# Spacing the weight halves between the chunk loads of a retention, soft-MoE and MLP kernel

## The chip, the cores and the metric

The kernel runs on one core of one Trainium2 chip. The metric is the device time of one execution in microseconds (us), the median of three runs; smaller is better. MB are 10^6 bytes, MiB 2^20.

## What is computed

Three layers follow each other on 4 x 768 = 3072 tokens of 512 features, all in 32-bit floats. The first is a retention layer of 8 heads of 64, written in the reference as a recurrence over time:

```python
for t in range(S):
    state = gamma[None, :, None, None] * state + np.einsum('bhd,bhe->bhde', k[:, :, t], v[:, :, t])
    y[:, :, t] = scale * np.einsum('bhd,bhde->bhe', q[:, :, t], state)
```

The second is a soft mixture of 8 experts with 4 slots each. Its logits are softmaxed over the tokens to make the slots' inputs, and over the slots to mix the experts' outputs:

```python
logits = x @ phi
d = softmax(logits, over tokens); slot_input = (d.T @ x).reshape(E, S_per_e, D)
slot_out[e] = np.maximum(slot_input[e] @ w1[e], 0.0) @ w2[e]
c = softmax(logits, over slots); x = c @ slot_out
```

The third is a plain MLP, `h = x @ w_in; g = h * sigmoid(1.702 h); out = g @ w_out`, with an inner width of 2048. The experts' weights `w1` (8 x 512 x 1024) and `w2` (8 x 1024 x 512) are 32 MiB together, by far the largest input.

## The kernel before

**The chunk loop.** The tokens are worked through in NI = 24 chunks of 128 (NC = 6 in each of 4 sequences). Chunk i has three inputs in DRAM: `ktv[i]` (k transposed and v, 512 KiB), `qt[i]` (q transposed, 256 KiB) and, for 12 of the chunks, `kt[i]` (k not transposed, 256 KiB; for the chunks in KTP the tensor engine transposes k itself, L221, and the last chunk of a sequence needs none). `stage_a` multiplies k by q (L210, tile sc), `stage_v` scales v on GpSimd (POOL), `stage_b` makes the chunk's output y from the running state and the chunk (L255, L259) and updates the state (L267), `stage_c` transposes the result (L280). Every fourth chunk closes a group, with logits (L312) and the token softmax. Iteration i of the loop runs `stage_a(i)`, `stage_b(i - 1)` and `stage_c(i - 2)`.

**The loads.** Nearly all transfers are issued by SyncE (SP), one after the other in program order, and an issue that has to wait for a buffer holds up everything behind it. Three sorts stand in that order: the chunk loads (`load_a(i + 2)` for ktv and qt, L185 and L187; `load_b(i + 1)` for kt, L199), the expert weights, and, later, the MLP's weights. `ktv` and `qt` have three buffers each, so that `qt[i + 2]` waits until the tensor engine has read `qt[i - 1]` in L255.

The expert weights come as 32 pieces of 1 MiB, in the order in which the experts use them: four pieces each of w1 of expert pair 0, w1 of pair 1, w2 of 0, w1 of 2, w2 of 1, w1 of 3, w2 of 2 and w2 of 3. 17 of these pieces (NW + NQ buffers, 14 and 3) are loaded during the chunk loop in 34 halves of 512 KiB (`load_half`, L123 and L128). The other 15 follow behind the loop (`load_piece`, L136; the very last in two halves again). Their buffers come free as the loop's tiles are closed and as the experts consume earlier pieces. Between the last ones stand the first halves of the MLP's `w_in` (L149) and `w_out` (L143).

How many halves each iteration issues, ahead of its own chunk loads, is set by one expression: in iteration i > 0, until `2 + i * 34 // 23` of them have been issued. That is three halves in iteration 1, then one or two in each, with the last one behind the loads of chunk 23.

**Behind the loop.** The slots' inputs are made (L475), then the four expert pairs run: `exp_w1` (L488, tile hp) and `exp_w2` (L513, tile eo), each 32 matmuls over four pieces. The last is `exp_w2(3)`, whose fourth piece is the last of the 32 to be loaded. Its result is copied out of PSUM in two halves, by ScalarE (L520) and VectorE (L521, tile os), transposed (L530, tile tq) and turned into the slots' outputs. From there the MLP runs on the tensor engine to the end (L644, L667, L730).

Of the kernel before, what the change touches and what calls it, by code (L numbers as in the profile page):

```python
# [24 lines left out]
NI = B * NC  # L25
# [8 lines left out]
NW = 14  # L34
NQ = 3
# [3 lines left out]
FULL = (2, 6, 7)  # L39
Q = 256  # L40
NWU = 3
I0 = 1
KTP = (0, 1, 2, 3, 8, 13, 16, 20)
BUD = 2.3
C1, C2 = 0.34, 0.6
# [4 lines left out]
def retention_soft_moe_mlp(  # L50
# [69 lines left out]
    def load_half(pool):  # L120
        if half:
            t, src = half.pop()
            nc.sync.dma_start(out=t[:, 2:4], in_=src[:, 2:4])  # L123
            return
        kind, e, k = pieces.pop()
        t = pool.tile([P, 4, 512], F32, tag="w", name=f"{kind}_{e}_{k}")
        src = (w1 if kind == "w1" else w2)[e, k].rearrange("p (j f) -> p j f", j=4)
        nc.sync.dma_start(out=t[:, 0:2], in_=src[:, 0:2])  # L128
        W[kind, e, k] = t
        half.append((t, src))  # L130
# [43 lines left out]
    def load_a(i):  # L174
        if i < NI:
            src = ktv[i].rearrange("p (a t) -> p a t", a=2)
            if i == 2:
                early.append(wp.tile([P, 4, 512], F32, tag="w", name="early"))
                ktv_t[i] = early[0][:, 0:2]
            else:  # L180
                ktv_t[i] = wt(f"ktv{i % 3}", [P, 2, 512], f"ktv{i}")
            if i < 2:
                nc.sync.dma_start(out=ktv_t[i][:, 0], in_=src[:, 0])
            else:
                nc.sync.dma_start(out=ktv_t[i], in_=src)  # L185
            qt_t[i] = wt(f"qt{(i + 1) % 3}", [P, NP, P], f"qt{i}")
            nc.sync.dma_start(out=qt_t[i], in_=qt[i].rearrange("p (a t) -> p a t", a=NP))  # L187
# [4 lines left out]
    def load_b(i):  # L192
        if i < NI and i % NC < NC - 1:
            if i == 3:
                t = early[0][:, i].rearrange("p (h d) -> p h d", h=H)
            else:
                t = wt(f"kt{(i - i // NC) % 3}", [P, H, D], f"kt{i}")
            if i not in KTP:
                nc.sync.dma_start(out=t, in_=kt[i].rearrange("p (h d) -> p h d", h=H))  # L199
            kt_t[i] = t  # L200
# [3 lines left out]
    def stage_a(i):  # L204
        q_, kv = qt_t[i], ktv_t[i]
        kT = kv[:, 0].rearrange("p (a t) -> p a t", a=NP)
        sc = [ps.tile([P, NP, P], F32, tag=f"sc{hh}", name=f"sc{hh}_{i}") for hh in range(2)]
        for a in range(NP):
            for hh in range(2):
                mm(sc[hh][:, a, :], lhsT=kT[hh * D:(hh + 1) * D, a, :], rhs=q_[hh * D:(hh + 1) * D, a, :],  # L210
                   start=True, stop=True)
        pt = [wt(f"pt{hh}{i % 2}", [P, NP, P], f"pt{hh}_{i}") for hh in range(2)]
        for hh in range(2):
            nc.vector.tensor_tensor(  # L214
                out=pt[hh], in0=sc[hh], in1=mask[:, None, :].to_broadcast([P, NP, P]), op=ALU.mult
            )
        p_t[i] = pt
        if i in KTP and i % NC < NC - 1:
            kp = ps.tile([P, NP, P], F32, tag="m", name=f"kp{i}", bufs=3)
            for a in range(NP):  # L220
                nc.tensor.transpose(kp[:, a, :], kT[:, a, :], ident)  # L221
            nc.scalar.copy(out=kt_t[i].rearrange("p h d -> p (h d)"), in_=kp.rearrange("p a t -> p (a t)"))

    def stage_v(i):
        c = i % NC
        v_ = ktv_t.pop(i)[:, 1].rearrange("p (h d) -> p h d", h=H)
        vt = wt(f"vt{i % 2}", [P, H, D], f"vt{i}")
        nc.gpsimd.tensor_tensor(
            out=vt, in0=v_, in1=vs[:, c, :, None].to_broadcast([P, H, D]), op=ALU.mult
        )  # L230
        vt_t[i] = vt
        if c == 0:
            tb_t[i] = tab
        else:
            tb_t[i] = wt("tb", [P, NP, P], f"tb{i}")
            nc.gpsimd.tensor_tensor(
                out=tb_t[i], in0=tab, in1=gsc[:, :, c, None].to_broadcast([P, NP, P]), op=ALU.mult
            )
# [3 lines left out]
    def stage_b(i):  # L242
        c = i % NC
        q_, vt, pt = qt_t.pop(i), vt_t.pop(i), p_t.pop(i)
        y = ps.tile([P, 2, 512], F32, tag="y", name=f"y{i}")

        def out_(a, hh):
            o = hh ^ (a & 1)
            return y[o * D:(o + 1) * D, a % 2, P * (a // 2):P * (a // 2) + P]

        if c > 0:
            for a in range(NP):
                for hh in range(2):
                    r = slice(hh * D, (hh + 1) * D)
                    mm(out_(a, hh), lhsT=s_sb[r, a, :], rhs=q_[r, a, :], start=(a < 2), stop=False,  # L255
                       skip_group_check=True)
        for a in range(NP):
            for hh in range(2):
                mm(out_(a, hh ^ (a & 1)), lhsT=vt[:, 2 * a + (hh ^ (a & 1)), :], rhs=pt[hh ^ (a & 1)][:, a, :],  # L259
                   start=(c == 0 and a < 2), stop=True, skip_group_check=True)  # L260
        if c < NC - 1:
            if c == 0:
                st_p[0] = ps.tile([P, NP, D], F32, tag="st", name=f"st{i}")
            st, k_ = st_p[0], kt_t.pop(i)
            for a in range(NP):
                for hh in range(2):
                    mm(st[hh * D:(hh + 1) * D, a, :], lhsT=k_[:, 2 * a + hh, :], rhs=vt[:, 2 * a + hh, :],  # L267
                       start=(c == 0 and a == 0), stop=True, skip_group_check=True)
            nc.scalar.copy(out=s_sb, in_=st)
        xT = xx.tile([P, NP, P], F32, tag="xT", name=f"xT{i}")  # L270
        nc.vector.tensor_tensor(
            out=xT.rearrange("p (s k) t -> p k s t", k=2), in0=y[:, :, 0:2 * P].rearrange("p k (s t) -> p k s t", s=2),
            in1=tb_t.pop(i).rearrange("p (s k) t -> p k s t", k=2), op=ALU.mult,
        )
        xT_t[i] = xT
# [23 lines left out]
    def stage_g1(g, part=False):  # L299
        if part in (True, False):  # L300
            lp = logits(g)
            if part:
                return lp
        else:
            lp = part
        softmax_stats(g, lp)
# [77 lines left out]
    def row_softmax(g):  # L384
        lp = ps.tile([P, 4, NS], F32, tag="m", name=f"rl{g}", bufs=3)
        nc.tensor.transpose(lp.rearrange("p j s -> p (j s)"), lT_t.pop(g), ident)
        rx = sm.tile([P, 4], F32, tag="rx", name=f"rx{g}")
        nc.vector.reduce_max(out=rx, in_=lp, axis=AX.X)
        ce = sm.tile([P, 4, NS], F32, tag="eT", name=f"ce{g}")
        nc.vector.tensor_tensor(out=ce, in0=lp, in1=rx[:, :, None].to_broadcast([P, 4, NS]), op=ALU.subtract)  # L390
        ex = sm.tile([P, 4, NS], F32, tag="ex", name=f"ex{g}", bufs=1)
        nc.scalar.activation(out=ex, in_=ce, func=AF.Exp)
        return ex
# [460 lines left out]
    with tc.manual_schedule():  # L854
# [18 lines left out]
        loaded = 0  # L873
        ex_t = {}
        for i in range(NI + 2):
            if i == 2:
                stage_b(1)
            if i < NI:
                stage_a(i)
                stage_v(i)  # L880
                while i > 0 and loaded < min(2 * (NW + NQ), 2 + i * 2 * (NW + NQ) // (NI - I0)):
                    load_half(wp if loaded < 2 * NW else wq)
                    loaded += 1
                load_b(i + 1)
                load_a(i + 2)
            if i >= 8 and i % 4 == 0 and i < NI:
                ex_t[i // 4 - 2] = row_softmax(i // 4 - 2)
            if i >= 9 and i % 4 == 1 and i < NI:
                row_norm(i // 4 - 2, ex_t.pop(i // 4 - 2))
            if 1 <= i <= NI and i != 2:  # L890
                stage_b(i - 1)
            if i >= 2:
                n = i - 1
                g = n // 4 - 1
                if i < NI + 1:
                    stage_c(i - 2)
                else:
                    lp = stage_g1(g, True)
                    stage_c(i - 2, True)
                    softmax_stats(g, lp)  # L900
                    combine1()
                    last_z = stage_g2(g)
                    stage_c2(i - 2)
                if n % 4 == 0 and i <= NI:
                    stage_g1(g)
                if n % 4 == 1 and n > 4:
                    stage_g2(g)
                if n % 4 == 2 and 4 < n < 22:
                    stage_g3(g)
# [337 lines left out]
```

## Time and profile before

| | us |
|---|---|
| median of three runs | 449.44 (449.42 to 450.48) |
| profiled execution, its own time | 451.76 |
| profiled execution, span from first to last instruction | 450.0 |
| tensor engine (PE) busy | 433.1 (96%) |
| VectorE / ScalarE / GpSimd busy | 333.4 / 205.3 / 47.9 |
| chunk loop, in that span | to about 115 |
| experts, in that span | about 121 to 159 |

The page divides the span in 40 slices of 11.25 us and gives for each the busy tenths of every engine, the tensor engine's granted clock and the rate of the DMA engines. The chain of waits is followed back from the last instruction, each step to what released it. A DMA in the chain lasts from its issue to its landing. All times "at 109.06" are us from the start of the span.

### The profile page before, as it was taken

The numbers are of one execution on the slowest core, as the hardware profiler recorded it, in microseconds if no ns is written. First come the engines' busy times: TensorE is split into PE (matmuls) and PEld (weight loads), VectorE is DVE, ScalarE is ACT, GpSimd is POOL, SyncE is SP. The second block draws the span as 40 slices with busy tenths as digits, with TensorE's granted clock in tenths as the row PEclk, the third lists the DMA queues.
The fourth block names the chain that finished last, engine by engine and source line by source line (L and its number), as shares of the span: only waits on it lengthen the run. The fifth ranks groups of instructions, "written<-read, shape, count | busy, mean of one in ns | idle before, by whom it ended". The sixth has DMA issues, their size and how long they took to land.

```text
span 450.0 us, 9917 instructions
## 1 busy us (share of the span) xinstructions
PE 433.1 (96%) x4105; PEld 359.9 (80%) x4105; DVE 333.4 (74%) x600; ACT 205.3 (46%) x351; POOL 47.9 (11%) x53
## 2 busy tenths in 40 slices
PE   8799998999999989999999999999999999999996
PEld 5687876877533367788888889999999999999995
DVE  2345665756456587987979689897797797988984
ACT  2232232322220166474656655655555555565530
POOL 3353543343100000000000000000000000000000
PEclk9999999999999999999999999999999999999999
DMA  8999999999899968687555502001301401311012
GB/s 300 407 365 408 389 371 407 344 407 325 328 411 411 380 228 281 182 299 268 181 194 188 184 5 94 1 1 47 129 14 47 141 1 49 140 48 46 23 74 93
DMA packets 27661, 92.38 MB, mean 205 GB/s; under 512 B 2864, under 2 KB 4288, under 8 KB 23264
## 3 DMA queue, kind: packets, MB, share of 16 engines
q1 hardware_dynamic: 27248, 91.24, 55.1%
q8 instruction: 32, 0.52, 0.5%
q10 hardware_dynamic: 288, 0.36, 0.3%
q0 software_dynamic: 80, 0.15, 0.1%
q14 instruction: 13, 0.11, 0.1%
HBM read 79.16 MB, written 12.58 MB: 204 GB/s over the span
## 4 chain that ended last, share of the span: by engine, by line
PE 81%; DMA 12%; DVE 3%; ACT 1%; issue 1%; POOL 1%; SPq 0%; DVEq 0%; POOLq 0%; ACTq 0%
PE P L730 35%; PE acc L667 18%; DMA qt<-qt_dram 10%; PE sc L210 4%; PE hb L696 4%; PE hp L488 3%; PE y L259 3%; PE eo L513 3%; PE y L255 2%; PE P L840 2%; PE xp L280 1%; PE op L370 1%; PE h L644 1%; DMA ktv_first<-ktv_dram 1%; PE st L267 1%
## 5 line engine op out<-in xcount | busy, mean ns | idle before, releaser
L691 DVE TENSOR_TENSOR forms<-forms 128x256 f32<-128x256 f32 (+1 forms) x93 | 47.6, 512 | 22.3 <-ACT forms L698 21.0
L698 ACT ACTIVATE forms<-hb 128x512 f32<-128x512 f32 x62 | 37.2, 599 | 54.7 <-PE hb L696 34.9
L667 PE MATMUL acc<-wo_hl,gh 128*128 128x512 f32 x192 | 59.8, 394 | 0.4 <-ACT gh L646 0.4
L730 PE MATMUL P<-bh,la 128*128 128x256 f32 x208 | 59.0, 284 | 0.0
L730 PE MATMUL P<-bl,ha 128*128 128x256 f32 x208 | 58.8, 283 | 0.0
L730 PE MATMUL P<-bh,ha 128*128 128x256 f32 x208 | 58.7, 282 | 0.0
L214 DVE TENSOR_TENSOR pt<-sc,ca_t 128x512 f32<-128x512 f32 x44 | 28.3, 685 | 24.5 <-PE sc L210 24.5
L730 PE MATMUL P<-bh,hs 128*128 128x256 f32 x156 | 44.1, 283 | 0.0
L730 PE MATMUL P<-bh,ls 128*128 128x256 f32 x156 | 44.1, 282 | 0.0
L730 PE MATMUL P<-bl,hs 128*128 128x256 f32 x156 | 44.0, 282 | 0.0
L667 PEld LDWEIGHTS acc<-wo_hl,gh 128*128 128x128 f32 x192 | 35.4, 188 | 8.1 <-issue 0.6
L730 PEld LDWEIGHTS P<-bl,ha 128*128 128x128 f32 x208 | 39.4, 189 | 1.2
L730 PEld LDWEIGHTS P<-bh,ha 128*128 128x128 f32 x208 | 39.4, 190 | 0.0
L730 PEld LDWEIGHTS P<-bh,la 128*128 128x128 f32 x208 | 39.4, 189 | 0.1
L691 DVE TENSOR_TENSOR la<-forms,ha 128x1024 fp32r<-128x1024 f32 x31 | 37.9, 1223 | 0.0
L667 PE MATMUL acc<-wo_hl,gl 128*128 128x512 f32 x96 | 37.4, 394 | 0.3 <-DVE gl L654 0.3
L714 ACT CAST ha<-forms 128x1024 fp32r<-128x1024 f32 x31 | 32.6, 1053 | 6.5 <-DVE forms L691 5.6
L646 ACT ACTIVATE gh<-h 128x512 fp32r<-128x512 f32 x30 | 18.0, 601 | 33.0 <-PE h L644 24.2
L714 ACT CAST hs<-forms 128x768 fp32r<-128x768 f32 x31 | 26.0, 839 | 10.1 <-DVE forms L691 7.5
L730 PEld LDWEIGHTS P<-bl,hs 128*128 128x128 f32 x156 | 29.5, 189 | 1.2
L210 PEld LDWEIGHTS sc<-qt,ktv 64*128 64x128 f32 x320 | 19.6, 187 | 13.1 <-issue 9.2
L210 PE MATMUL sc<-qt,ktv 64*128 64x128 f32 x320 | 23.2, 284 | 6.6 <-DMA qt<-qt_dram 6.6
(224 smaller groups left out, 925.2 us busy)
## 6 DMA issues: line engine op xcount, KB each, us to landing
w<-w_dram SPq DMA_DIRECT2D x36, 512.0 KB, 7.7
w<-w_dram SPq DMA_DIRECT2D x14, 1024.0 KB, 8.3
ktv<-ktv_dram SPq DMA_DIRECT2D x20, 512.0 KB, 8.3
wi<-w_in_dram SPq DMA_DIRECT2D x7, 1024.0 KB, 5.5
wo<-w_out_dram SPq DMA_DIRECT2D x7, 1024.0 KB, 4.9
parts<-stage SPq DMA_DIRECT2D x24, 256.0 KB, 2.9
pt<-parts SPq DMA_DIRECT2D x6, 1024.0 KB, 4.8
qt<-qt_dram SPq DMA_DIRECT2D x21, 256.0 KB, 6.5
```

What stands on the lines that cost most here:

```text
L210: mm(sc[hh][:, a, :], lhsT=kT[hh * D:(hh + 1) * D, a, :], rhs=q_[hh * D:(hh + 1) * D, a, :], start=True, stop=True)
L214: nc.vector.tensor_tensor(out=pt[hh], in0=sc[hh], in1=mask[:, None, :].to_broadcast([P, NP, P]), op=ALU.mult)
L259: mm(out_(a, hh ^ (a & 1)), lhsT=vt[:, 2 * a + (hh ^ (a & 1)), :], rhs=pt[hh ^ (a & 1)][:, a, :], start=(c == 0 and a < 2), stop=True, ski ...
L488: mm(hp[32 * j:32 * j + 32, :], lhsT=slotT[:, k, SPE * (j // 2):SPE * (j // 2) + NS], rhs=w[:, j, :], start=(k == 0), stop=(k == KDM - 1))
L513: mm(op[32 * j:32 * j + 32, :], lhsT=hT[:, kk, 32 * j:32 * j + 32], rhs=w[:, j, :], start=(kk == 0), stop=(kk == 3))
L646: nc.scalar.activation(out=gh, in_=hp, func=AF.Gelu_apprx_sigmoid)
L667: mm(acc[t], lhsT=g[:, t * P:(t + 1) * P], rhs=w, start=f == f0 and n == 0, stop=f == f1 and n == 2)
L691: nc.vector.tensor_tensor(out=out_, in0=a, in1=b_, op=op)
L696: mm(PB["h"], lhsT=gst[:, f * P:(f + 1) * P], rhs=cT[:, 512 * b:512 * b + 512], start=True, stop=True)
L698: nc.scalar.activation(out=t[:, 3 * a:3 * a + 2].rearrange("p s d -> p (s d)"), in_=PB["h"], func=AF.Gelu_apprx_sigmoid)
L714: nc.scalar.copy(out=AH[n, k], in_=FT[0][:, c0:c1])
L730: mm(PB[p][:, t], lhsT=g[:, c], rhs=w, start=r == span_[b][0] and t == 0 and i == 0, stop=r == span_[b][1] - 1 and i == 2, skip_group_chec ...
```

## The change

One constant takes the place of another (I0 = 1 goes, NHW = 26 comes), and the expression that says how many halves have been issued by iteration i is a new one:

```diff
-I0 = 1
+NHW = 26
...
-                while i > 0 and loaded < min(2 * (NW + NQ), 2 + i * 2 * (NW + NQ) // (NI - I0)):
+                while loaded < (NHW * i // (NI - 3) if i < NI - 2 else 2 * (NW + NQ)):
                     load_half(wp if loaded < 2 * NW else wq)
                     loaded += 1
                 load_b(i + 1)
                 load_a(i + 2)
```

So 26 halves are spread evenly over iterations 1 to 21 (one in iteration 1), and the remaining eight are issued together in iteration 22, which has no chunk loads of its own any more. The number of transfers, their sizes, their order among the weights and every instruction of the other engines stay as they are; only SP's order differs.

SP's order at the front, before, from the load of chunk 2 (`early`, a weight buffer that is borrowed for it) to that of chunk 5 (`w_0_0` is a piece of w1 of pair 0; ktv_173 and qt_175 belong to chunk 3, ktv_251 and qt_253 to chunk 4, qt_292 to chunk 5):

```order
L185 DMA early<-ktv_dram 128x1024
L187 DMA qt_first<-qt_dram 128x512
L128 DMA w_0_0_168<-w_dram 128x1024
L123 DMA w_0_0_168<-w_dram 128x1024
L128 DMA w_0_1_171<-w_dram 128x1024
L185 DMA ktv_173<-ktv_dram 128x1024
L187 DMA qt_175<-qt_dram 128x512
L123 DMA w_0_1_171<-w_dram 128x1024
L185 DMA ktv_251<-ktv_dram 128x1024
L187 DMA qt_253<-qt_dram 128x512
```

The same place of SP's order after the change (chunk 3 is now ktv_170 and qt_172, chunk 4 ktv_248 and qt_250):

```order
L185 DMA early<-ktv_dram 128x1024
L187 DMA qt_first<-qt_dram 128x512
L128 DMA w_0_0_168<-w_dram 128x1024
L185 DMA ktv_170<-ktv_dram 128x1024
L187 DMA qt_172<-qt_dram 128x512
L123 DMA w_0_0_168<-w_dram 128x1024
L185 DMA ktv_248<-ktv_dram 128x1024
L187 DMA qt_250<-qt_dram 128x512
```

One half instead of three stands ahead of chunk 3, two instead of four ahead of chunk 4.

SP's order at the last chunk, before (qt_1570 is chunk 23's; the first L136 is the first whole piece behind the loop):

```order
L123 DMA w_2_3_1494<-w_dram 128x1024
L128 DMA w_1_0_1564<-w_dram 128x1024
L199 DMA kt_1566<-kt_dram 128x512
L185 DMA ktv_1568<-ktv_dram 128x1024
L187 DMA qt_1570<-qt_dram 128x512
L123 DMA w_1_0_1564<-w_dram 128x1024
L136 DMA w_1_1_1855<-w_dram 128x2048
```

The same place after the change (chunk 23 is ktv_1557 and qt_1559):

```order
L128 DMA w_2_0_1552<-w_dram 128x1024
L123 DMA w_2_0_1552<-w_dram 128x1024
L199 DMA kt_1555<-kt_dram 128x512
L185 DMA ktv_1557<-ktv_dram 128x1024
L187 DMA qt_1559<-qt_dram 128x512
L128 DMA w_2_1_1651<-w_dram 128x1024
L123 DMA w_2_1_1651<-w_dram 128x1024
L128 DMA w_2_2_1654<-w_dram 128x1024
L123 DMA w_2_2_1654<-w_dram 128x1024
L128 DMA w_2_3_1657<-w_dram 128x1024
L123 DMA w_2_3_1657<-w_dram 128x1024
L128 DMA w_1_0_1660<-w_dram 128x1024
```

Eight halves instead of one now stand between chunk 23's loads and the first whole piece: seven halves fewer are ahead of the last chunk, and seven more behind it.

## Rows read from the trace of the kernel before

**Rows 1.** Waits of the tensor engine to 180 us: total us, times, longest.

```profile
PE sc L210 <- DMA qt<-qt_dram: 6.6, 6, 1.8
```

**Rows 2.** Stretches: us, busy of PE, PEld, DVE, ACT, POOL, PEclk, DMA share, GB/s.

```profile
0.00:109.00 109.00, 100.13 (x1635) 79.72 (x1635) 57.91 (x115) 31.16 (x77) 44.77 (x49) 1.00 1.00 378
20.00:100.00 80.00, 76.07 (x1309) 61.57 (x1309) 45.92 (x92) 23.94 (x61) 32.56 (x32) 1.00 1.02 385
109.00:125.00 16.00, 15.09 (x201) 9.07 (x201) 6.94 (x19) 2.90 (x9) 2.17 (x4) 1.00 0.84 303
125.00:157.00 32.00, 31.71 (x275) 10.84 (x268) 19.22 (x63) 4.84 (x9) 0.95 (x1) 1.00 1.01 402
160.00:180.00 20.00, 18.44 (x118) 14.41 (x119) 15.83 (x31) 13.05 (x27) 0.00 (x0) 1.00 0.77 263
```

**Rows 3.** Tensor engine in order of time, last chunks: start, us, instruction, [idle before].

```profile
104.15 1.16 PE L210 MATMUL sc<-qt,ktv 64*128 64x128 f32 x16
105.24 0.67 PE L255 MATMUL y<-qt,s_sb 64*64 64x128 f32 x16
105.84 1.09 PE L259 MATMUL y<-pt,vt 128*64 128x128 f32 x16
106.76 0.64 PE L267 MATMUL st<-vt,kt 128*64 128x64 f32 x16
107.33 0.66 PE L280 MATMUL xp<-cb_t,xT 128*128 128x128 f32 x4
107.82 0.27 PE L358 MATMUL ep<-cb_t,eT 128*128 128x128 f32 x1
109.06 1.16 PE L210 MATMUL sc<-qt,ktv 64*128 64x128 f32 x16 [0.97 <-DMA qt<-qt_dram]
```

**Rows 4.** Chain of waits at the last chunk: start, us, what.

```profile
100.54 0.64 PE y L255 x16
101.18 0.02 issue
101.19 7.78 DMA qt<-qt_dram
108.97 0.09 issue
109.06 1.16 PE sc L210 x16
```

**Rows 5.** Transfers of tile qt, the 21 behind the first three.

```profile
DMA to landing us min/median/max: 4.1/6.5/8.4
```

**Rows 6.** SP in order of time, the last expert weights: start, us, issue.

```profile
137.95 0.50 SPq L136 DMA_DIRECT2D w<-w_dram  x1
...
138.98 0.42 SPq L136 DMA_DIRECT2D w<-w_dram  x1
139.45 0.42 SPq L128 DMA_DIRECT2D w<-w_dram  x1
139.92 1.27 SPq L123 DMA_DIRECT2D w<-w_dram  x1
```

**Rows 7.** Issue to landing (last number, us) of the pieces issued at 137.95 and 138.98.

```profile
w<-w_dram SPq DMA_DIRECT2D x1, 1024.0 KB, 10.2
...
w<-w_dram SPq DMA_DIRECT2D x1, 1024.0 KB, 13.1
```

**Rows 8.** The same of the last half, issued at 139.92.

```profile
w<-w_dram SPq DMA_DIRECT2D x1, 512.0 KB, 15.3
```

**Rows 9.** Chain of waits through the last expert pairs.

```profile
148.10 3.61 PE eo L513 x32
...
152.43 1.06 PE eo L513 x8
153.50 0.60 PE tq L530 x4
...
154.68 0.35 DVE wfb L162
...
157.15 0.69 DVE wo_hl L592
157.85 0.34 DVE os L521
158.19 0.04 issue
158.24 0.44 PE tq L530 x2
158.67 0.30 PE cp L423 x4
158.97 0.98 PE gd L551 x8
```

**Rows 10.** Tensor engine in order of time, the last three pieces' reader.

```profile
154.02 2.78 PE L513 MATMUL eo<-w,hT 128*32 128x512 f32 x24
```

**Rows 11.** Waits of the tensor engine from 160 us on, all.

```profile
PE hb L696 <- ACT forms L698: 0.7, 1, 0.7
PE h L644 <- DVE gst L557: 0.7, 1, 0.7
PE acc L667 <- ACT gh L646: 0.4, 1, 0.4
PE acc L667 <- DVE gl L654: 0.3, 1, 0.3
PE rp0b L576 <- DVE Gl L568: 0.2, 1, 0.2
```

**Rows 12.** SP's issue of the second part of w_in, and its issue to landing.

```profile
141.71 0.38 SPq L149 DMA_DIRECT2D wi<-w_in_dram  x1
...
wi<-w_in_dram SPq DMA_DIRECT2D x1, 512.0 KB, 15.0
```

**Rows 13.** VectorE in order of time, the first use of that part.

```profile
159.08 0.43 DVE L162 TENSOR_SCALAR win<-wi 128x512 uint32<-128x512 uint32 x1
```

## The prediction

> **What bounds the kernel now.** I read the tensor engine's waits first. Up to 180 us it waits for a transfer in one place only: six times for a chunk's qt, 6.6 us in all, 1.8 at most [rows 1]. The last of the six is the 0.97 us in front of chunk 23 [rows 3]; elsewhere in the loop its instructions follow each other without a gap, as the rows ahead of it show, so that without those waits the loop would run at the tensor engine's own pace. From 160 us on it waits 2.3 us in all [rows 11], so time that is won ahead of 160 should reach the end.
>
> Then the stretches [rows 2]. The DMA engines are the other thing that is full: share 1.00 to 1.02 at 378 to 385 GB/s through the chunk loop, and 1.01 at 402 GB/s from 125 to 157 us. The one thinner stretch is 109 to 125 us, 0.84. The queue carries the chunk loads and the expert weights together, so the qt waits are the price of the weights ahead of them. It stays full until the last expert weight, issued at 139.92 [rows 6], lands 15.3 us later, at 155.2 [rows 8].
>
> Last the chain at the experts' end [rows 9]. The last 24 matmuls of eo start at 154.02 [rows 10] and take 0.11 us each (32 in 3.61 us), so the four that read the last half start at about 156.3, 1.1 us after it landed. And they are not the last thing either: the copy that reads them (os, L521) stands at 157.85 because VectorE is still narrowing an MLP weight (wfb to wo_hl, 154.68 to 157.84). The second pair of transposes (tq) follows at 158.24. That time is what I forecast: it is the join behind which everything is the tensor engine's.
>
> **The change, part by part.**
>
> *Seven halves leave the stretch ahead of chunk 23.* They are 7 x 0.524 = 3.67 MB, which at 378 GB/s is 9.7 us of the queue. By the queue alone qt of chunk 23, which lands at 108.97 [rows 4], would be there at 99.3. But it is issued only when L255 of chunk 20 has read its buffer, at 101.19, 0.02 us after it. Five of the six waits lie ahead of that, 6.6 - 1.0 = 5.6 us, so the issue moves to 95.5. A qt takes 4.1 to 8.4 us to land, 6.5 in the middle [rows 5]; with a thinner queue I take 5, so it lands at 100.5 (99.6 to 103.9). The tensor engine wants it at 109.06 - 6.6 = 102.4. So I count all six waits as gone: the loop is 6.6 us shorter, and the queue, now ahead of the tensor engine, runs dry for 100.5 - 99.3 = 1.2 us. That is about as much as it lost before in the thin stretch, where 16 us at 303 instead of 385 GB/s are 3.4 us at the most.
>
> *The same seven halves, and with them every later piece, stand behind chunk 23.* Between the landing of its qt and that of the last expert weight lay one half, 15 pieces and a half each of w_in and w_out, 16.5 MiB or 17.3 MB; they took 46.3 us. Now it is 20 MiB or 21.0 MB. At 402 GB/s that is 52.2 us, at the 385 of the loop 54.5, and at the 374 that the whole tail had (17.3 MB in 46.3 us, thin stretch included) 56.1. The thin stretch should fill up, since eight halves (10 us) are queued ahead of the whole pieces that waited there for their buffers. But the 402 counts what all DMA engines moved, while a piece has landed only when the slowest has; I take 385, which the loop held over 80 us. Last weight: 100.5 + 54.5 = 155.0, against 155.2 before. The ends are 99.6 + 52.2 = 151.8 and 102.4 + 56.1 = 158.5.
>
> *So the tensor engine arrives early and waits.* Its eo of pair 3 would start at 152.43 - 6.6 = 145.8. The pieces landed before at 148.2 and 152.1 [rows 6, 7], and the last at 155.2; they come at nearly those times again, while it wants them at 147.4, 148.3 and 149.2. I expect it to stand there three times, for 1 to 2 us, about 3 us and 2 us. What was a wait for qt becomes a wait for w2 of pair 3.
>
> *What is left* is the slack at the join. VectorE's narrowing runs while the tensor engine waits, so the copy no longer queues behind it. After the last half lands at 155.0: four matmuls 0.45, 0.1 to the copies, a copy 0.35, the first pair of transposes 0.3, and the second pair starts at 156.3 with the issue times between (0.1). Before it was 158.24. The gain is 1.9 us. With the ends above it is 5.1 us and -1.6 us.
>
> *Free of charge:* SP issues as many transfers as before and the other engines' instructions are untouched; SP's eight issues in a row take 0.4 us each, and no chunk load stands behind them. The first w_in and w_out parts keep their place behind the same weights. The second part of w_in landed at 156.7, 1.5 us behind the last weight [rows 12], and is first used at 159.08 [rows 13], 0.8 us behind the join; now that is 156.5 and 157.1, a cover of 0.6 us, and what it were late beyond that would be added.
>
> The profiled span of 450.0 us becomes 448.1, its run of 451.76 becomes 449.9. The same 1.9 us off the median of 449.44 is **447.5 us**. About 0.3%, 1.35 us, is what a measurement of this kernel can tell from no change.
>
> **The rivals.** *The weights keep up.* If the full queue has all pieces there by the time the tensor engine wants them, the six waits are simply saved: 449.44 - 6.6 = 442.8. It needs the last half at 149.2 instead of 155.0, that is 21.0 MB in 49 us, 430 GB/s; the best stretch has 402. A part of it, up to the 5.1 us above, is possible.
>
> *The loop does not speed up, and the queue idles instead.* If something else sets the loop's pace once qt is early (POOL's v, ScalarE's copy of the state, ktv), qt of chunk 23 still waits for its buffer, the queue stands empty meanwhile, and the 20 MiB start late. It decides at 102.4 for that landing: 102.4 + 54.5 = 156.9, join at 158.2, nothing gained. With half of the 5.6 us of waits replaced by others, qt lands at 103.3, the last weight at 157.8, join 159.1, 0.9 us slower; with all of them replaced at 106.1 and 160.6, 3.7 us slower, 453.1. Against it speaks that between the waits the tensor engine runs without a gap [rows 3].
>
> *The clock falls.* The longest wait in the trace is 1.8 us, and the granted clock is 1.00 in all stretches [rows 2]. The three waits of up to 3 us with only 0.9 us of matmuls between are something the trace does not show. If the clock fell there to the lower of its two levels, the matmuls behind would take twice as long until it rose; of 20 us behind the join 18.4 are tensor work [rows 2], so 3 us at that level cost up to 3 us less what lies beside other work. I take 2.5: 447.5 + 2.5 = 450.0. The Trainium skill (TensorE: Matmul & The Clock Gate, section "HAM oscillation — how this bites in real kernels") says that short bursts of matmuls between DMA waits let the clock gate close again. By that rule this rival would be the likely one, 450.0; no row here shows such a fall.
>
> *The change does not do what it says*: SP's order shows that it does.
>
> **How the numbers follow.** The weights gate and a gain of 0.4 to 3.9 us is left: 0.68, of which 0.50 lie beyond 0.3% and 0.18 within. A larger gain: 0.09. The loop's pace is set by something else: 0.15, of which 0.07 within 0.3% and 0.08 slower. The clock falls: 0.08, half of it within and half slower. Faster 0.59, same 0.29, slower 0.12. The range from 445.5 (3.9 us gained) to 450.0 (half of the waits replaced, or the clock) leaves out 0.09 below and about 0.1 above.
>
> **What would show it.** In the changed profile the six qt waits are gone or small and chunk 23's sc starts near 102.5; the DMA share is about 1.0 from 97 to 157 us, with no thin stretch at 109 to 125; eo of pair 3 waits for w some 5 to 6 us in all; the second tq pair is near 156.3. I am wrong if qt of chunk 23 lands after 102, if the last weight lands far from 155, or if the granted clock dips at 145 to 160.

## The result, and the profile after

The changed kernel takes **452.3 us** (median of 7 runs, 451.39 to 455.11) against 450.48 for the kernel before in the same comparison (449.42 to 452.24): a ratio of 1.0055, 95% interval 1.003 to 1.0081. It is 0.55% slower; 447.5 was forecast, and 450.0 was the end of the range. Its profiled execution took 452.3 us, with a span of 450.5. The ratios of the experiments leave out five disturbed executions (455.2 to 2358.5 us); their medians include them, which moves none by more than 0.25 us.

The tensor engine's waits up to 180 us (total us, times, longest) in the changed kernel:

```profile
PE sc L210 <- DMA qt<-qt_dram: 2.8, 3, 1.1
PE eo L513 <- DMA w<-w_dram: 2.7, 3, 2.3
```

Of the 6.6 us of waits for qt [rows 1] 2.8 are left, and 2.7 us of waits for weights are new. The stretches of the changed kernel, columns as in [rows 2]:

```profile
0.00:109.00 109.00, 103.98 (x1700) 83.03 (x1701) 59.61 (x118) 31.14 (x77) 45.59 (x49) 1.00 0.96 352
20.00:100.00 80.00, 77.20 (x1338) 62.76 (x1336) 46.65 (x95) 23.40 (x60) 33.90 (x33) 1.00 0.98 360
109.00:125.00 16.00, 15.15 (x160) 7.26 (x159) 6.79 (x22) 3.21 (x10) 1.30 (x3) 1.00 1.02 419
125.00:157.00 32.00, 29.01 (x242) 9.31 (x241) 18.51 (x59) 4.64 (x8) 0.95 (x1) 1.00 1.02 412
```

The thin stretch at 109 to 125 us has filled up (share 0.84 to 1.02, 303 to 419 GB/s), as forecast. But the loop has become thin instead: 0.96 and 352 GB/s up to 109 us, where it was 1.00 and 378. The granted clock is 1.00 throughout. The tensor engine in order of time (start, us, instruction, [idle before]):

```profile
105.67 1.16 PE L210 MATMUL sc<-qt,ktv 64*128 64x128 f32 x16
...
117.50 1.09 PE L475 MATMUL sp<-sb,A 128*128 128x32 f32 x8 [0.63 <-DVE A L378]
...
150.62 1.06 PE L513 MATMUL eo<-w,hT 128*32 128x512 f32 x8
153.94 1.06 PE L513 MATMUL eo<-w,hT 128*32 128x512 f32 x8 [2.25 <-DMA w<-w_dram]
155.22 1.05 PE L513 MATMUL eo<-w,hT 128*32 128x512 f32 x4 [0.21 <-DMA w<-w_dram]
156.51 1.05 PE L513 MATMUL eo<-w,hT 128*32 128x512 f32 x4 [0.24 <-DMA w<-w_dram]
...
158.09 0.90 PE L530 MATMUL tq<-cb_t,os 128*128 128x128 f32 x4
```

Chunk 23's sc starts at 105.67, not 109.06 [rows 3]: the loop won 3.4 us, and the first work behind it (L475) stands at 117.50 where it was at 120.89 in the kernel before:

```profile
120.89 1.09 PE L475 MATMUL sp<-sb,A 128*128 128x32 f32 x8 [0.63 <-DVE A L378]
```

At 150.62 + 1.06 the engine has caught up with the weights and waits. The chain of waits there (start, us, what):

```profile
123.69 17.44 DMA w<-w_dram
141.15 15.32 DMA w<-w_dram
156.47 0.04 issue
156.51 1.08 PE eo L513 x4
157.63 0.04 issue
157.67 0.38 ACT os L520
158.05 0.04 issue
158.09 0.44 PE tq L530 x2
158.55 0.44 PE tq L530 x2
```

The last half is issued at 141.15 and lands at 156.47, where it landed at 155.2 before [rows 6, 8]. From there the last four matmuls, the copy and the first pair of transposes lead to the second pair at 158.55; before it was 158.24 [rows 9]. So the tensor engine lost all of its 3.4 us again, and 0.3 more.

**Everything behind that pair costs the same in every profile used here.** An execution's time less the start of the second tq pair is 451.76 - 158.24 = 293.5 us before and 452.30 - 158.55 = 293.75 after, and between 293.3 and 293.8 in the others. What has to be explained is the pair's place. And the profiled execution of before was one of its longer ones (451.76, median 450.48): a typical one has its pair at 450.5 - 293.5 = 157.0, 1.5 us ahead of the changed kernel's. That is most of the 1.8 us between the medians.

### The profile page after: what moved, and what is told of

Read it like the earlier page. It is cut to its first block, busy times and chain, and to the rows that moved or that the text cites. A ratio compares the mean times of both kernels' runs of the same rounds, so it can differ in the third digit from the quotient of the medians.

```text
span 450.5 us, 9919 instructions
## 1 busy us (share of the span) xinstructions
PE 435.2 (97%) x4105; PEld 360.2 (80%) x4105; DVE 333.7 (74%) x600; ACT 205.3 (46%) x351; POOL 47.8 (11%) x53
## 4 chain that ended last, share of the span: by engine, by line
PE 82%; DMA 12%; DVE 3%; ACT 1%; issue 1%; POOL 0%; DVEq 0%; SPq 0%; POOLq 0%; ACTq 0%
PE P L730 34%; PE acc L667 18%; DMA w<-w_dram 7%; DMA qt<-qt_dram 5%; PE sc L210 5%; PE y L259 4%; PE hb L696 4%; PE y L255 2%; PE xp L280 2%; PE P L840 2%; PE st L267 2%; PE op L370 1%; PE h L644 1%; PE wu L870 1%; PE hp L488 1%; PE kp L221 1%
## 5 line engine op out<-in xcount | busy, mean ns | idle before, releaser
L698 ACT ACTIVATE forms<-hb 128x512 f32<-128x512 f32 x62 | 37.1, 599 | 54.5 <-PE hb L696 34.0
L691 DVE TENSOR_TENSOR la<-forms,ha 128x1024 fp32r<-128x1024 f32 x31 | 37.9, 1223 | 0.0
L730 PEld LDWEIGHTS P<-bh,hs 128*128 128x128 f32 x156 | 29.5, 189 | 0.0
L691 DVE TENSOR_TENSOR ls<-forms,hs 128x768 fp32r<-128x768 f32 x31 | 29.5, 951 | 0.0
```

The costliest lines, as they stand in the source:

```text
L691: nc.vector.tensor_tensor(out=out_, in0=a, in1=b_, op=op)
L698: nc.scalar.activation(out=t[:, 3 * a:3 * a + 2].rearrange("p s d -> p (s d)"), in_=PB["h"], func=AF.Gelu_apprx_sigmoid)
L730: mm(PB[p][:, t], lhsT=g[:, c], rhs=w, start=r == span_[b][0] and t == 0 and i == 0, stop=r == span_[b][1] - 1 and i == 2, skip_group_chec ...
```

## The experiments

The letters for theories in the texts on record do not mean the same from one group of runs to the next; go by their words and numbers. Three explanations were to be told apart: **the end of the queue** (the last weight sets the time, and each half that is moved behind the loop costs its own bytes there), **the loop** (it does not get shorter, because something other than the halves sets its pace, or the queue idles) and **the clock**. Unless another diff stands there, a kernel is the changed one with another number of halves spread over iterations 1 to 21; the rest of the 34 is issued behind chunk 23:

```diff
-NHW = 26
+NHW = 22        # nhw22; 27, 28, 30, 32 in the others
```

**The front alone, and the back alone.** `front_only` is the kernel before with one half instead of three in iteration 1; `behind_only` is the changed kernel with three at the front and still eight behind.

```diff
 # front_only, against the kernel before
-while i > 0 and loaded < min(2 * (NW + NQ), 2 + i * 2 * (NW + NQ) // (NI - I0)):
+while i > 0 and loaded < min(2 * (NW + NQ), (0, 1, 2, 4, 6)[i] if i < 5 else 2 + i * 2 * (NW + NQ) // (NI - I0)):
 # behind_only, against the changed kernel
-while loaded < (NHW * i // (NI - 3) if i < NI - 2 else 2 * (NW + NQ)):
+while loaded < (max((0, 3, 4, 4, 4)[min(i, 4)], NHW * i // (NI - 3)) if i < NI - 2 else 2 * (NW + NQ)):
```

> The front alone is thinned: one half ahead of chunk 3 instead of three (1, 2, 4, 6 halves issued by iterations 1 to 4 instead of 3, 4, 6, 7), from iteration 5 on the schedule of the kernel before, one half behind chunk 23. Theory A (up to the last expert weight the transfers are one full queue, and the end follows the landing of the last weight): the 1.8 us wait of chunk 3 goes, but the other qt waits grow by as much, qt of chunk 23 lands at 109 and the last weight at 155 as before; the time is that of before within 0.7 us. Theory B (what an early qt wins stays won, and only the eight halves behind cost): about 1.8 us faster than before. Theory C (the run-to-run scatter of the transfers is larger than any effect of the order): no difference either.

> The eight halves behind chunk 23 alone: the front as before (three halves ahead of chunk 3, four by iteration 2), then nothing until the even schedule of 26 has caught up in iteration 5. Theory A: as the changed kernel, 1 to 2.5 us slower than before, last weight at 156 to 157, with the qt wait of chunk 3 back (1.8 us) and the other waits smaller. Theory B: slower than the changed kernel by 1.8 us. Theory C: no difference from before beyond 0.5 us.

Measured: `front_only` 455.32 us, ratio 1.0126 (1.0092 to 1.016); `behind_only` 452.38 us, 1.0077 (1.0042 to 1.0112). The back alone gives the whole loss, as theory A has it (its chunk 3 waits 0.6 us for qt, not 1.8). The front alone is worse still, which none of its three theories has. Its first 20 us, the same 20 us of the kernel before, and 3.5 us around its chunk 7:

```profile
0.00:20.00 20.00, 17.77 (x188) 12.13 (x188) 7.02 (x11) 4.78 (x8) 7.58 (x12) 1.00 0.87 306
37.50:41.00 3.50, 3.38 (x30) 3.18 (x32) 1.29 (x2) 0.00 (x0) 1.53 (x2) 0.51 1.04 406
```

```profile
0.00:20.00 20.00, 15.96 (x169) 11.39 (x170) 6.04 (x10) 4.28 (x7) 7.64 (x12) 1.00 0.92 347
```

With fewer halves to start on, the queue moves 0.8 MB less in 20 us (306 against 347 GB/s). The halves that it lacks come two and three at a time in iterations 3 to 5. Chunk 7 then waits 3.16 us, the longest wait in any profile of the loop, and behind it the clock is at its lower level (0.51). That the bunched halves cause this wait is not shown: `nhw26_again`, which has no such bunch, waits 2.08 us at the same chunk. The mean granted clock of all its six runs was 0.991 to 0.996, so that a part of this kernel's loss is probably the clock's.

```profile
37.62 2.08 PE L210 MATMUL sc<-qt,ktv 64*128 64x128 f32 x16 [3.16 <-DMA qt<-qt_dram]
```

**More halves behind, and fewer.**

> 22 halves spaced over the chunk loads and twelve behind the last chunk. Theory A: the loop can gain at most the 2.8 us of qt waits that are left with 26, so the tail, longer by 2.1 MB or 5.1 us at 412 GB/s, starts at most 2.8 us earlier: last weight at 158.5 to 161, 2 to 5 us slower than the changed kernel. If the queue was not what the end waits for (theory C): as the changed kernel within 0.7 us.

> 30 halves spaced over the chunk loads and four behind the last chunk, instead of 26 and eight. Theory A: four halves (5 us of queue) are just enough to fill the thin stretch at 109 to 125 us (2.6 us of idle queue), and the loop's queue runs dry for less than with 26 (3.4 us there); the last weight lands at 154 to 155.5 and the tensor engine arrives with it; 0.5 to 1.5 us faster than before. Theory C: no difference from before.

Measured: `nhw22` (12 behind) 456.54 us, 1.0142 (1.0118 to 1.0167); `nhw30` (four behind) 448.28 us, 0.9951 (0.9927 to 0.9976), faster than both kernels, and by more than the 0.5 to 1.5 us expected; its profile is that of `nhw30_again` below. `nhw22` is 4.2 us above the changed kernel, as theory A has it (its last weight lands at 158.1, issued at 142.76). It has no wait for qt at all, and in its place:

```profile
PE eo L513 <- DMA w<-w_dram: 6.8, 4, 2.2
```

```profile
151.79 1.63 PE L513 MATMUL eo<-w,hT 128*32 128x512 f32 x8 [2.19 <-DMA w<-w_dram]
155.57 4.02 PE L513 MATMUL eo<-w,hT 128*32 128x512 f32 x16 [2.15 <-DMA w<-w_dram]
```

Its L475 starts at 114.06, 6.8 us ahead of before:

```profile
114.06 1.09 PE L475 MATMUL sp<-sb,A 128*128 128x32 f32 x8 [0.63 <-DVE A L378]
```
That is the tensor engine's own pace, the loop that I forecast for 26; it is worth nothing, since its second tq pair comes at 160.6. Here the clock falls too (second row, 0.51, from 152 us on):

```profile
145.00:152.00 7.00, 3.39 (x28) 1.31 (x32) 2.47 (x8) 0.59 (x1) 0.00 (x0) 1.00 1.03 404
152.00:159.00 7.00, 4.85 (x22) 0.71 (x16) 2.81 (x6) 0.62 (x1) 0.00 (x0) 0.51 1.03 397
```

**The last weights taken out of the race.** Both kernels without the loads of the four w2 pieces of pair 3; exp_w2(3) reads those of pair 2 instead. These kernels leave out four MiB of transfers and compute the last pair with another pair's w2.

```diff
+if kind == "w2" and e == 3:
+    W[kind, e, k] = W["w2", 2, k]
+    return
...
-        load_half(wp)
-        load_half(wp)
+        load_piece(wp)
```

> The kernel before with the same four pieces left out (w2 of pair 2 read in their place, the result is not the reference's). Theory A: the last weight is not what the end waits for there (VectorE's narrowing and the tensor engine arrive 1 us after it), so the time is that of the kernel before within 0.7 us. If the end hung on the transfers there too: 2 us or more faster.

> The changed kernel without the loads of the last four expert pieces (w2 of pair 3, 4 MiB); the matmuls that read them read w2 of pair 2 instead, so the result is not the reference's. Theory A (the last weight's landing sets the end in the changed kernel): the waits for w (2.7 us there) are gone, the tensor engine reaches the last eo 3.4 us earlier than in the kernel before and nothing holds it; 3 to 4 us faster than the changed kernel, some 2 us faster than the kernel before. If the end hung on something else: as the changed kernel within 0.7 us.

Measured: on the kernel before 450.08 us, 0.9994 (0.9962 to 1.0026); on the changed one 448.58 us, 0.9952 (0.992 to 0.9985). So the last weights cost the kernel before nothing that can be measured, and the changed one 1% (1.0055 to 0.9952), some 4 us. The forecast's main claim, that a wait for w2 of pair 3 takes the place of the waits for qt, is shown. But without that wait the shorter loop is worth about 1.9 us (0.9994 to 0.9952), not 6.6, and the two intervals overlap, so that even these 1.9 us are not clear of the noise.

**The clock held up.** Two unused 512-column matmuls between the second and third piece of the last pair, in the changed kernel.

```diff
-exp_w2(3, 1, 4)
+exp_w2(3, 1, 2)
+hold(2)          # 2 x mm(keep, lhsT=ident, rhs=<a landed piece>)
+exp_w2(3, 2, 4)
```

> The changed kernel with two extra matmuls of 512 columns, whose result is not used, in the gap in which the tensor engine waits for the third piece of w2 of pair 3. Theory D (in about half of the changed kernel's runs the granted clock falls in these waits, 0.992 to 0.996 in the mean instead of 0.999, and those runs are up to 3 us longer): all runs have a mean clock of 0.998 or more, the time is 0.3 to 1.5 us below the changed kernel's and its scatter smaller. If the clock is not the cause of the scatter: no difference, or up to 1 us slower for the extra matmuls.

Measured: 451.95 us, 1.0022 (0.9993 to 1.0052). Its interval overlaps that of the changed kernel, so a gain is not shown. The mean granted clock was 0.998 or more in all but one of its runs, and ten of these still spread from 449.43 to 454.02 us: runs differ by that much without any fall of the clock. What a fall costs, the experiment could not show: in the one profile of the changed kernel that has a fall (`nhw26_again`, below) it lies in the loop, at chunk 7, where the two extra matmuls do nothing.

Its profiled execution, the shortest of its runs (449.43), shows something else. SP's order in the loop is the changed kernel's, and this time the loop went as forecast:

```profile
95.91 0.33 SPq L187 DMA_DIRECT2D qt<-qt_dram  x1
115.21 1.09 PE L475 MATMUL sp<-sb,A 128*128 128x32 f32 x8 [0.63 <-DVE A L378]
```

qt of chunk 23 is issued at 95.91 (95.5 was forecast), L475 comes 5.7 us ahead of before, and the second tq pair stands at 155.96 (156.3 was forecast). So the forecast loop is one that this order can have, and not the one that it has as a rule.

**Between 26 and 33.**

> The kernel with 30 halves among the chunk loads and four behind once more, for its profile and a second measurement. Theory A: 0.3 to 0.8% faster than before again; the last weight lands at 153 to 155, the tensor engine waits for w less than 1 us and for qt 2.5 to 5 us; DMA share over 0.97 at 109 to 125 us.

> 28 halves among the chunk loads, six behind the last chunk. Theory A2 (the loop stops getting shorter somewhere near 30, and from there every half that is moved behind it costs its own 1.3 us at the end): between the kernels with 30 (448.2) and 26 (452.3), 449.5 to 451.5, the last weight landing 1.5 to 3 us later than with 30. If the cost came from the thin front or from the clock and not from the halves behind: as with 30 or as with 26, not between.

> 32 halves among the chunk loads, two behind the last chunk. Theory A2: here the chunk loop is the limit again, its qt waits grow (4 to 6 us instead of 2 to 3 with 30) and the last weight no longer matters; 0 to 2 us slower than with 30, at or below the kernel before (449 to 450.5). If only the halves behind mattered: as with 30 or faster.

> 30 halves and four behind as in nhw30, but with three halves ahead of chunk 3 as in the kernel before (3, 4, 4, 5 issued by iterations 1 to 4 instead of 1, 2, 4, 5). Theory A2 with a front that idles the queue: the early qt wait returns (1 to 2 us) but the later ones shrink by as much or more, since the queue moves 0.8 MB more in the first 20 us; as nhw30 within 0.7 us, at best 1 us faster. If an early qt that lands early is a gain that stays: 1 to 2 us slower than nhw30.

> The kernel before, unchanged, for a second profile. The first profiled execution took 451.76 us where the median of its timed runs is 449.5 to 450.5. If the scatter lies in the transfers of the chunk loop: the six qt waits together are less than 6.6 us by about what the time is shorter, and everything from the second pair of tq to the end takes the same 291.7 us.

Measured: `nhw30_again` 448.07 us, 0.9949 (0.9916 to 0.9983); `nhw28` 447.54, 0.9938 (0.9913 to 0.9963); `nhw32` 449.72, 0.9964 (0.993 to 0.9999); `nhw30_front` (30, with `behind_only`'s three halves at the front) 449.53, 0.9971 (0.994 to 1.0003); `before_again`, one run, 450.85. The front makes no difference that can be measured at 30 either (0.9949 and 0.9971, with intervals that overlap).

`before_again` has 5.2 us of waits for qt, as expected for a shorter run. Three expectations missed. In `nhw30_again` the waits for qt are 2.1 us, not 2.5 to 5. In `nhw32` they are 1.9 us, not 4 to 6; its time came out as expected, but its profile, that of its shortest run, does not show the reason given. And `nhw28` is not between 30 and 26: 28 and 30 can't be told apart (0.9938 and 0.9949). For that outcome its text names the thin front or the clock as what 26 pays for. The front it is not, since `behind_only` has the front of before and loses as much; nor is it the clock alone, since of the runs with a mean clock of 0.998 or more those of `nhw26_again` have a median of 451.56 us and those of both kernels with 28 of 447.55. From 28 to 26 the time jumped by 4.8 us, where 2 x 0.524 MB at the tail's 412 GB/s are 2.5. The last three runs, on one chip, were for that jump.

> The changed kernel once more, on one chip with 27 and 28 spaced halves. Theory A (the end of the queue sets the time: each half that is not spread over the loop adds its own 0.524 MB at the tail's 412 GB/s, 1.3 us): 2.5 us above 28 spaced halves, 450 us if those are at 447.5. Theory B (below 28 something more is lost, since the queue idles in the loop, and a spell of slow transfers there is then no longer made up): 4 to 5 us above 28 spaced halves, 452, with a wider spread.

> 27 halves spread over iterations 1 to 21, seven behind the last chunk. Theory A: midway, 1.3 us above 28 spaced halves. Theory B: 2 us or more above them.

> 28 spaced halves, six behind, once more: both theories 447.5 (447 to 449), 0.6% faster than the kernel before; it shows whether the earlier time of this version holds. In the profile: waits for qt under 2 us, waits for w under 1 us, the last weight landing near 151.5 to 153.

Measured: `nhw26_again` 452.13 us, 1.0049 (1.0021 to 1.0078); `nhw27` 450.61, 1.0000 (0.9971 to 1.0029); `nhw28_again` 447.55, 0.9939 (0.9916 to 0.9962). From 28 to 26 that is 4.6 us (4.9 by the ratios): the jump is real, and more than the bytes of two halves, as theory B has it. How it divides between the first half that is moved behind and the second (3.1 and 1.5 us by the medians, 2.7 and 2.2 by the ratios) is within the noise. All kernels of the row, from their profiles (the stretch is 20 to 105 us). A profile is of one execution, whose time stands in the third column; those of `nhw22`, `hold_clock`, `nhw27` and `nhw32` are 1.2 to 2.5 us below their kernel's median:

| halves spread / behind | median us, ratio | profiled, us | share, GB/s | L475 at | waits for qt / w | second tq pair |
|---|---|---|---|---|---|---|
| 22 / 12 | 456.54, 1.0142 | 454.15 | 0.97, 347 | 114.06 | 0 / 6.8 | 160.59 |
| 26 / 8 (the change) | 452.30, 1.0055 | 452.30 | 0.97, 359 | 117.50 | 2.8 / 2.7 | 158.55 |
| 26 / 8 again | 452.13, 1.0049 | 453.49 | 0.96, 354 | 119.32 | 3.7 / 2.0 | 159.71 |
| 26 / 8, `hold_clock` | 451.95, 1.0022 | 449.43 | 1.01, 372 | 115.21 | 0.6 / 0.5 | 155.96 |
| 27 / 7 | 450.61, 1.0000 | 448.57 | 1.01, 375 | 115.23 | 0.3 / 1.6 | 155.20 |
| 28 / 6 | 447.54, 0.9938 | 447.01 | 1.01, 385 | 114.92 | 0.8 / 0.4 | 153.51 |
| 28 / 6 again | 447.55, 0.9939 | 447.60 | 1.01, 384 | 116.33 | 1.8 / 0 | 154.18 |
| 30 / 4 again | 448.07, 0.9949 | 448.18 | 1.02, 389 | 117.46 | 2.1 / 0 | 154.80 |
| 32 / 2 | 449.72, 0.9964 | 448.52 | 1.03, 397 | 117.73 | 1.9 / 0 | 155.08 |
| before | 450.48 | 451.76 | 1.02, 384 | 120.89 | 6.6 / 0 | 158.24 |
| before again | 450.85 | 450.85 | 1.02, 387 | 119.98 | 5.2 / 0 | 157.32 |

(The pair of 22 / 12 is the first pair's 160.13 and the 0.46 us that lie between the two pairs in the changed kernel's chain.) The rows of that stretch in `nhw26_again`, `nhw27` and `nhw28_again`, in this order:

```profile
20.00:105.00 85.00, 81.83 (x1404) 66.64 (x1402) 50.46 (x102) 25.13 (x66) 35.91 (x35) 0.98 0.96 354
```

```profile
20.00:105.00 85.00, 84.73 (x1489) 69.18 (x1481) 51.63 (x106) 26.42 (x70) 37.71 (x37) 1.00 1.01 375
```

```profile
20.00:105.00 85.00, 83.11 (x1449) 67.66 (x1447) 51.14 (x104) 26.25 (x69) 37.00 (x37) 1.00 1.01 384
```

And up to 105 us, the changed kernel and `nhw28_again`:

```profile
0.00:105.00 105.00, 99.98 (x1631) 79.56 (x1631) 57.38 (x114) 30.02 (x74) 43.54 (x47) 1.00 0.96 350
```

```profile
0.00:105.00 105.00, 100.86 (x1643) 80.50 (x1645) 58.16 (x115) 31.11 (x77) 44.58 (x49) 1.00 0.99 369
```

Up to 105 us the changed kernel has moved 350 x 105 = 36.8 MB, `nhw28_again` 38.7, the kernel before 377 x 105 = 39.6. All of them move the same bytes before the last half lands, so what is missing at 105 us is moved behind it. Against `nhw28_again` that is 2.0 MB, nearly twice the two halves (1.05 MB) that the schedule took away; at 412 GB/s it is 4.8 us, and the pair lies 4.4 us later. So in this execution the jump is time in which the queue did not move bytes in the loop. Two things lie in it: with 26 the DMA engines are idle more (share 0.96 against 0.99), and while they are busy they are slower (359 / 0.97 = 370 GB/s, against 384 / 1.01 = 380).

Not every execution with 26 is like that. The same two stretches of `hold_clock`'s:

```profile
0.00:105.00 105.00, 102.01 (x1671) 81.45 (x1673) 59.10 (x117) 31.10 (x77) 45.54 (x49) 1.00 0.99 361
20.00:105.00 85.00, 84.23 (x1475) 68.60 (x1473) 52.08 (x106) 26.25 (x69) 37.95 (x37) 1.00 1.01 372
```

Here the share is as high as with 28, 0.8 MB less than in `nhw28_again` has moved by 105 us (361 x 105 = 37.9 MB), and the pair is 1.8 us later than there, 2.4 later than in `nhw28`: no more than the bytes of the two halves (2.5 us) account for. What the usual execution with 26 loses beyond these bytes goes with a loop that is held up on the way, and what holds it up in some executions and not in others is not shown.

## Why the prediction was wrong

**The mechanism was right, and its balance was not.** The waits for qt went over into waits for w2 of pair 3, the thin stretch filled up, the last weight became what gates, and the clock stayed at 1.00 in the profile. In the terms of the sum, this failed.

**1. "So I count all six waits as gone."** This is the step that failed. Its waits were not all gone, and qt of chunk 23 landed at 105.46, not 100.5, which was the forecast's first sign of being wrong:

```profile
34.63 1.16 PE L210 MATMUL sc<-qt,ktv 64*128 64x128 f32 x16 [1.02 <-DMA qt<-qt_dram]
69.79 1.16 PE L210 MATMUL sc<-qt,ktv 64*128 64x128 f32 x16 [0.64 <-DMA qt<-qt_dram]
88.39 1.16 PE L210 MATMUL sc<-qt,ktv 64*128 64x128 f32 x16 [1.13 <-DMA qt<-qt_dram]
98.84 0.33 SPq L187 DMA_DIRECT2D qt<-qt_dram  x1
```

It was issued at 98.84, not 95.5, because 2.8 us of waits for qt (chunks 7, 15 and 19) were left ahead of it, and it was 6.6 us on the way, not 5. The step behind both is that fewer halves ahead make a qt land sooner: in the changed kernel the 21 transfers of qt take 6.4 us in the median (3.7 to 8.4), where they took 6.5 [rows 5] (6.1 in `nhw26_again`, 5.6 in `hold_clock`, 5.0 in `nhw22`). Even in the executions whose loop went as forecast, chunk 23's took 6.3 us or more (7.1 in `hold_clock`, 6.3 in `nhw22`). The forecast's own range for the landing ended at 103.9, although the upper end of its time was worked out from 102.4. The loop won 3.4 us in this profile, 1.6 in `nhw26_again` (119.32) and 5.7 in `hold_clock`'s (115.21): it can be nearly as short as forecast, but is not reliably so. I had subtracted the seven halves' queue time from a queue that would run dry for 1.2 us. Measured is a share of 0.96, which leaves 4% of 109 us, 4.4 us, idle, with waits for qt in the same loop. My reading of how both can be is this, and no run tests it: SP can't issue the next qt until L255 has read its buffer, so that a queue that has run dry has nothing ahead, and when transfers then go through slowly for a while, the tensor engine waits although the queue was idle shortly before.

**2. The rival that came nearest** is the second, "the loop does not speed up, and the queue idles instead", to which I gave 0.15. It decided at 102.4 for the landing of chunk 23's qt, and with all waits replaced it had 106.1. That outcome came, but its cause did not: no other engine sets the pace, and 2.8 of the 3.2 us that the loop did not win are waits for qt again. I set against it that the tensor engine runs without a gap between its waits [rows 3]. That is true, and `nhw22` shows the floor, 6.8 us below. But the argument says only what the tensor engine could do, nothing of what the queue does with the time. The comparison that I left out: a chunk needs 4.28 us of the tensor engine (in `nhw22` sc of chunk 3 starts at 16.61 and that of chunk 23 at 102.22). With 26 / 21 halves per iteration the loop asks for 0.65 MB of weights per chunk, and `nhw28`'s loop carries 28 / 21, 0.70 MB, at nearly that pace (L475 at 114.92) and a share of 1.01. So the loop had room for more than 26, and each byte that is not moved in it is paid for at the end.

**3. The tail was faster than I took it.** 20 MiB in 156.47 - 105.46 = 51.0 us are 411 GB/s, where I took 385 (and 402 as the better end). This gave back 3.5 us of the 5.0 that the late start cost. 105.46 + 54.5 would have been 160.0.

**4. Behind the last half** the second pair comes 158.55 - 156.47 = 2.1 us later, not 1.3: the last four matmuls take 1.08 us in the chain to where the copy can start, not 4 x 0.11. My 0.11 came from a full stream [rows 9]; here the last four take as long as the eight that start behind the wait at 153.94 (1.05 and 1.06 us). Why is not shown.

**5. The base.** 6.6 us of waits were those of one execution, and a longer one than usual: 451.76 us, where I subtracted its gain from a median of 449.44. `before_again` has 5.2, and `now23_before`'s profile 2.1. So there was less to win than the page showed.

With the measured terms the sum is 105.46 + 51.0 + 2.1 = 158.6, 0.3 us behind before's profiled 158.24; the rest of the 1.8 us between the medians is the base. Of the 4.8 us between the forecast of 447.5 and the measured 452.3, 2.25 lie in the pair's place (158.55, not 156.3) and 0.2 behind it; the other 2.3 are the base, since the profiled execution of before lay 1.3 us above its median of 450.48, and this median 1.0 above the 449.44.

**The clock** (0.08) did not decide, but it was there. The mean clock of the changed kernel's seven runs was 0.992 to 0.999, and in `nhw26_again` the four runs at 0.996 or less had spans of 451.5 to 453.9 us, the other eight 448.6 to 451.3. In the profile of `nhw26_again` the fall follows a wait of 2.08 us at chunk 7:

```profile
35.13 1.83 PE L210 MATMUL sc<-qt,ktv 64*128 64x128 f32 x16 [2.08 <-DMA qt<-qt_dram]
35.10:42.00 6.90, 6.87 (x77) 5.48 (x77) 2.67 (x4) 0.96 (x2) 2.48 (x3) 0.75 0.92 345
```

All 24 runs of the two kernels with 28 are at 0.999 or 1.00 and span 444.8 to 447.8. The Trainium skill (TensorE: Matmul & The Clock Gate, section "HAM oscillation — how this bites in real kernels") says that waits for DMAs between bursts of matmuls close the gate. `nhw22` and `front_only` agree (0.51 behind such waits); the changed kernel's single wait of 2.25 us at 153.9 did not do it (1.00). The runs with a lower clock are no proof that the clock causes the longer spans, since a longer wait lengthens a run by itself. And at full clock the loss is still there: the changed kernel's three runs at 0.999 took 451.39 to 452.3 us.

**What stays open:** why transfers go slower in the loop when fewer weights stand between the chunk loads (358 GB/s per unit of share with 22, 370 with 26, 380 with 28, 385 with 32, and 376 to 379 before, with 33), and why the loop's waits differ so much between executions of one order. The waits for qt come at every fourth chunk in the kernel before (3, 7, 11, 15, 19, 23; in `before_again` at 5, 7, 11, 15, 16, 19 and 23) and at chunks 7, 15 and 19 in the changed one. Whether it is the smaller loads, their addresses or their timing was not tried; nor was a fourth buffer for qt, which would let SP issue it earlier.

## What to carry to other kernels

When loads that are needed later fill the gaps of a loop, two limits must be set against each other: the bytes that the loop's own pace leaves room for, and the bytes that have to come behind it. What could have moved in the loop and did not comes back at the end; more than fits makes the loop wait. Here 28 of 34 was the lowest point (447.5 us, 0.6% faster than before), not to be told from 30, and the curve is steeper towards fewer (4.6 us from 28 to 26) than towards more (2.2 us from 28 to 32). A forecast from one profile also needs to know how far executions of the same order lie apart: here that was more than what was to be won. When a wait disappears, follow the queue as well as the engine that waited: ask what the queue does with the time.

## What the runs showed of the hardware

The same queue moves 347 to 397 GB/s in the chunk loop (20 to 105 us, share 0.96 to 1.03) and 412 to 419 behind it in the changed kernel (109 to 157 us, share 1.02): the share says how long the engines are occupied, not how fast. The Trainium skill (DMA: Bandwidth & Descriptors, section "Where 436 GB/s comes from") has about 358 GB/s as the limit between HBM and SBUF for one core and 435 for the fabric; 419 GB/s from 109 to 125 us lies above the first, which therefore did not bind this one core, and below the second. And the end of the loop lay up to 4.1 us apart in profiled executions with the same order of issue (L475 at 117.50 and 119.32 in the changed kernel, 115.21 in `hold_clock`), which is more than the effect that was to be forecast.
